# mLSTM cell followed by a leaky-ReLU MLP, in float32: the second product of the last group but one is computed by the same 26 block products as the last group's

## The chip, the cores and the metric

The kernel runs on one core of one Trainium2 chip. The time is the device time of one launch in microseconds (us). A core has TensorE (PE in the profile, its weight loads PEld), VectorE (DVE), ScalarE (ACT), GpSimd (POOL) and SyncE (SP, which only issues DMAs here). Each engine takes its instructions strictly in program order and they wait for one another through semaphores.

## The reference

```python
batch, n_heads, seq, head_dim = 4, 8, 768, 40        # q, k, v, o_gate; i_gate, f_gate without head_dim
for t in range(S):                                    # mLSTM cell
    m_new  = max(f_t + m, i_t); f_stab = exp(f_t + m - m_new); i_stab = exp(i_t - m_new); m = m_new
    C = f_stab * C + i_stab * outer(v_t, k_t)
    n = f_stab * n + i_stab * k_t
    y_t = sigmoid(o_t) * (C @ q_t) / max(abs(n . q_t), 1)
x = y as (3072 tokens, 320)                           # batch and time, heads and head_dim
h = x @ w_in                                          # 320 -> 2048
out = maximum(0.01 * h, h) @ w_out                    # 2048 -> 320
```

All data are float32.

## The kernel before

**Groups and stages.** The 768 time steps are cut into six chunks of 128. Chunk c of the four batches makes four *cells* (s = 4c to 4c + 3) and, afterwards, group c of the MLP: 512 tokens, one block of 128 per batch. The main loop (line 1471 onwards) runs stage c = 1 to 6: the MLP *units* of group c - 1 (`ffs = ff_units(c - 1)`), one per step i, and between them, at steps written out by hand, the pieces of the cells of chunk c. Stage 6 has no cells. So group 4's MLP runs beside the cells 20 to 23, and group 5's alone. All orders on TensorE, VectorE, ScalarE and GpSimd are those of the program text (`manual_schedule`).

**First product of a group** (`fast_firsts`, 14 units): x times w_in by seven products of half-size blocks (Winograd's form of Strassen's scheme) in two halves n each, in the order p1, p6, p7, p4, p2, p5, p3. The result of p1, p6, p7 is copied out by ScalarE (`keep`, line 1066); p2, p5, p3 add their PSUM banks to it on VectorE (`add`, line 1062, two instructions of 128x512 a unit), then ScalarE applies the leaky ReLU in place (`relu`, line 1058). p5 and p3 of a half share their PSUM banks: p3 goes on accumulating in them after p5's `add` has read them. The tiles of PSUM come from two pools of four banks, `psf` and `psc`, each handed round in order. The input sums for the next group (`sums_of_x`, line 1015, four on GpSimd) stand at the end of each stage.

**Second product.** Groups 1 to 4 use `fast_units`: 14 units, seven products of 8 float32 block matmuls in two halves, in all 112 of 128x128 by 128x160, each recorded as two (224 records). Group 5 uses `last_units`: activations in 4x4 blocks (a00 to a33, 512 rows of features, one batch), w_out in 4x2 blocks (b00 to b31, 512 by 160), output 4x2 (c00 to c31), and 26 products P0 to P25 instead of 32, each 4 block matmuls: 104 in all, 208 records. A text table says what each unit does: B are sums of blocks of w_out, A sums of activations, N and c the accumulations of the products. Two-operand lines go to VectorE (`nc.vector.tensor_tensor`, lines 1238 and 1246), a line that copies a product goes to ScalarE (1241, 1243). In group 5 the 18 sums B0 to B17 (128x640 each) are made by VectorE in the units 0 to 7 of the first product, after one instruction (line 1256) that adds back a half of w_out that Strassen's scheme had replaced by a difference.

**A cell of chunk 5** has two pieces on TensorE: `u_parts` (scores, matmuls of lines 725 and 731; then on VectorE four multiplications, line 742, and a state addition, 705) and `u_mix` (matmuls of line 813 into a bank pT; then on VectorE a transpose, line 820, three small denominators and a multiply, line 824; on GpSimd a multiply, line 827; on VectorE a second transpose, line 831; four DMAs to `x_dr`, and later `gather_x`, which reads them back as the next group's xT). Ahead of `u_parts`, VectorE transposes k and q (`prep_kq`, line 604, two instructions) and multiplies (line 612, two instructions). These four are taken from the generator `fine[s]`, one per unit. GpSimd makes a scaled state (701) and scaled k (567) per cell in `ahead`.

In stage 5, `pairs = (-1, -1, 3, 3, 13, 13, 17, 17, 17)` places the pieces: `u_parts` of cells 20 and 21 ahead of unit 0, their `u_mix` after unit 3, `u_parts` of 22 and 23 after unit 13, that is after the first product, and their `u_mix` after unit 17, inside the second.

Of the kernel before, what the change touches and what calls it, by code (L numbers as in the profile page):

```python
# [18 lines left out]
def kernel(  # L19
# [28 lines left out]
    P = 128  # L48
# [753 lines left out]
    def u_mix(s):  # L802

        c, b = divmod(s, B)
        d = st[s]
        prep_o(s)
        pT = psc.tile([P, PR * P], F32, name="pT", tag="c")
        S, m = S_t[s % NL], mixed(s)
        for u in range(2):
            for j in range(PR):  # L810
                for r in range(2):
                    h = 2 * j + r
                    nc.tensor.matmul(  # L813
                        pT[DP * r : DP * (r + 1), j * P + u * SL : j * P + (u + 1) * SL], lhsT=S[:, u, h, :],
                        rhs=m[:, u, h, :], start=True, stop=True,
                    )
        if c + 1 < NB:
            state_next(s, 1)
        hb = wk.tile([P, PR * TB, QW], F32, name="hb", bufs=1)
        nc.vector.transpose(hb[:].rearrange("p (j n) d -> p j n d", n=TB), in_blocks(pT[:]))  # L820
        den = wk.tile([P, PR * TB], F32, name="den")
        denominators(den[:], hb[:, :, DB])
        x3 = xb[:, :, :DB]
        nc.vector.scalar_tensor_tensor(  # L824
            x3, in0=raw_blocks(s, 2, DB), scalar=1.0, in1=hb[:, :, :DB], op0=ALU.add, op1=ALU.mult,
        )
        nc.gpsimd.tensor_tensor(x3, x3, den[:].unsqueeze(2).to_broadcast([P, PR * TB, DB]), op=ALU.mult)  # L827
        if c + 1 < NB:
            state_add(s, 1)
        xq = wk.tile([P, PR * P], F32, name="x")  # L830
        nc.vector.transpose(in_blocks(xq[:]), xb[:].rearrange("p (j n) d -> p j n d", n=TB))
        to = x_dr[s].rearrange("(j n i) t -> n i j t", n=4, i=DB)
        for n in range(4):
            sync.dma_start(to[n], xq[QW * n : QW * n + DB].rearrange("p (j t) -> p j t", t=P))
        del st[s]
# [30 lines left out]
    def ff_units(g):  # L866
# [45 lines left out]
        if g == NB - 1:  # L912
            return last_units(g, fast_firsts(g))
# [103 lines left out]
    def fast_firsts(g):  # L1017
# [94 lines left out]
    LAST_ROWS, LAST_KS = (0, 2, 1, 3), (1, 2, 0, 3)  # L1112
    LAST_EARLY = {
# [13 lines left out]
    }  # L1127
    LAST = (
# [26 lines left out]
    )  # L1155

    def last_units(g, firsts):
# [5 lines left out]
        lo = raw_l[:, : 3 * KH * NH]  # L1163
# [3 lines left out]
        flat = [t[:].rearrange("p n h d -> p (n h d)") for t in (kn, qn)]  # L1167
        flat += [t[:].rearrange("p u h d -> p (u h d)") for t in S_t]
        r_l = [t[:].rearrange("p u w -> p (u w)") for t in rb_t]
        sums_b = [lo[:, n * NW : (n + 1) * NW] for n in range(6)]  # L1170
        sums_b += [t[:, n * NW : (n + 1) * NW] for t in flat[:2] + r_l for n in range(3)]
        sums_b += [t[:, :NW] for t in flat[2:]]
        sums_a = [w_all[:, n, :AW] for n in range(NL)] + [t[:, :AW] for t in sums_b[18:]]
        del sums_b[18:]
        sums_a += [xb[:].rearrange("p n d -> p (n d)")]
        sums_c = [t[:, NW + n * NH :][:, :NH] for t in flat[2:] for n in range(2)] + p1_at
        behind = [w_all[:, n, AW:] for n in range(NL)]
        behind += [w_in[:, n, m * AW : (m + 1) * AW] for n in range(QN) for m in range(2)]
        text = "; ".join([LAST_EARLY[n] for n in sorted(LAST_EARLY)] + list(LAST))
        words = [w.strip("-") for w in text.replace(";", " ").split()]  # L1180
        left = {w: words.count(w) for w in words}
        spare = {"A": sums_a, "B": sums_b, "N": sums_c}
        tiles = {}

        def name(w):
# [3 lines left out]
            if kind == "a":  # L1189
                m, n = LAST_ROWS[int(rest[0])], LAST_KS[int(rest[1])]  # L1190
                return acts[:, 4 * n : 4 * n + 4, ts(m, P)]
            if kind == "b":
                n = LAST_KS[int(rest[0])]
                return w_out[:, 4 * n : 4 * n + 4, ts(int(rest[1]), NH)]
            if kind == "c":
                m = LAST_ROWS[int(rest[0])]
                return rows[m][:, ts(int(rest[1]), NH)]
# [3 lines left out]
            else:  # L1201
                got = spare[kind].pop(0)
                tiles[w] = got if kind == "N" else got.rearrange("p (f d) -> p f d", f=4)
            return tiles[w]

        def used(*ws):
            for w in ws:
                left[w] -= 1
                if left[w] == 0 and w[0] == "A":
                    spare["A"].append(tiles[w].rearrange("p f d -> p (f d)"))  # L1210
                if left[w] == 0 and w[0] == "N":
                    spare["N"].append(tiles[w])
# [5 lines left out]
        def send(w):  # L1218
            m, d = LAST_ROWS[int(w[1])], int(w[2])
            if w[:2] != "c2":  # L1220
# [4 lines left out]
            else:  # L1225
                cols = ts(d, NH)
            sync.dma_start(out[m * S + g * P : m * S + (g + 1) * P, cols], rows[m][:, cols])

        def do(line):
            to, op, *ws = line.split()  # L1230
            signed, ws = ws[0], [w.strip("-") for w in ws if w not in ("+", "-", "*")]
            src = [name(w) for w in ws]
            if op == "=" and " * " in line:
                bank = name(to)
                for f in range(4):
                    nc.tensor.matmul(bank, lhsT=src[0][:, f, :], rhs=src[1][:, f, :], start=f == 0, stop=f == 3)  # L1236
            elif len(src) == 2:
                nc.vector.tensor_tensor(name(to), src[0], src[1], op=ALU.add if " + " in line else ALU.subtract)
            elif op == "=":
                if signed[0] == "-":  # L1240
                    nc.scalar.activation(name(to), src[0], AF.Copy, scale=-1.0)
                else:
                    nc.scalar.copy(name(to), src[0])
            else:
                z = name(to)
                nc.vector.tensor_tensor(z, z, src[0], op=ALU.add if op[0] == "+" else ALU.subtract)
            used(to, *ws)

        def run_lines(lines):
            for line in lines.split(";"):  # L1250
                do(line.strip())

        def ahead_of(n):
            firsts[n]()
            if n == 0:
                nc.vector.tensor_tensor(low_w[:, :, NH:], low_w[:, :, NH:], low_w[:, :, :NH], op=ALU.add)
            if n in LAST_EARLY:
                run_lines(LAST_EARLY[n])

        def product(n):  # L1260
            if n == 0:
                sums_a.extend(behind)
            run_lines(LAST[n])

        return [lambda n=n: ahead_of(n) for n in range(len(firsts))] + [lambda n=n: product(n) for n in range(len(LAST))]
# [167 lines left out]
    with tc.manual_schedule(engines={E.PE, E.DVE, E.Activation, E.Pool}):  # L1433
# [31 lines left out]
        pairs = (-1, -1, 3, 3, 13, 13, 17, 17, 17)  # L1465
# [125 lines left out]
```

## Time and profile before

| what | value |
|---|---|
| median of 3 runs | 471.49 us (470.62 to 472.23) |
| the profiled execution | 471.96 us, of which the span of its instructions 470.2 us |
| PE busy | 459.6 us (98% of the span) |
| PEld busy | 412.5 us (88%) |
| DVE busy | 365.4 us (78%) |
| ACT busy | 206.6 us (44%) |
| POOL busy | 170.1 us (36%) |
| granted TensorE clock | 1.00 |

Times inside the text count from the start of the span. Stage 5 lies between 337.6 us (first `u_parts`) and 407.4 us; stage 6 from there to the end. A busy time is the union of an engine's instructions, and idle time of an engine that nobody waits for costs nothing; what matters is which wait ends last at each step of the chain.

### The profile page before, as it was taken

How to read it: one execution, taken by the hardware profiler on the slowest of the kernel's cores; microseconds unless marked ns; L12 is line 12 of the kernel's file. 1: busy time of each engine (PE TensorE's matmuls, PEld its weight loads, DVE VectorE, ACT ScalarE, POOL GpSimd, SP SyncE). 2: the span in 40 equal slices, each digit the busy share in tenths (PEclk: the TensorE clock that was granted, in tenths of full speed). 3: DMA queues.
4: the chain of work that ended last, by engine and by line, in shares of the span. 5: the costliest groups of instructions: out<-in, count | busy, mean ns of one | idle time of the engine just before them, and what ended most of it. 6: DMA issues, size and time to landing. Idle time of an engine off the chain costs nothing.

```text
span 470.2 us, 14195 instructions
## 1 busy us (share of the span) xinstructions
PE 459.6 (98%) x5700; PEld 412.5 (88%) x5700; DVE 365.4 (78%) x676; ACT 206.6 (44%) x507; POOL 170.1 (36%) x219
## 2 busy tenths in 40 slices
PE   8988989999999999999999999999999999999997
PEld 5777878767788999988899988899988899988997
DVE  6778578998579999768689778689757687495886
ACT  4657878755337511356411367411356411153410
POOL 6230487264335154933214933214833004400000
PEclk9999999999999999999999999999999999999999
DMA  9999977878742594865654956654776213100001
GB/s 128 169 179 179 214 181 230 207 158 164 147 141 55 151 181 107 186 141 134 166 133 84 197 127 140 179 110 100 176 142 125 75 30 85 57 1 1 1 1 56
DMA packets 160849, 59.21 MB, mean 126 GB/s; under 512 B 123792, under 2 KB 152208, under 8 KB 160784
## 3 DMA queue, kind: packets, MB, share of 16 engines
q1 hardware_dynamic: 120800, 51.15, 49.3%
q10 hardware_dynamic: 39984, 7.17, 9.3%
q8 instruction: 45, 0.74, 0.7%
q14 instruction: 20, 0.16, 0.1%
HBM read 51.58 MB, written 6.70 MB: 124 GB/s over the span
## 4 chain that ended last, share of the span: by engine, by line
PE 88%; DMA 5%; SPq 3%; POOL 1%; issue 1%; ACT 0%; DVE 0%; POOLq 0%; DVEq 0%
PE ph L1033 33%; PE po L931 26%; PE po L894 8%; PE pl L1236 6%; PE pT L813 3%; SPq L95 3%; PE ph L872 3%; PE sd L725 3%; DMA kn<-in_k_dram 3%; DMA acts<-in_moe_w_in_dram 1%; DMA w<-a_dr 1%; PE sd L731 1%; PE tk L638 1%; PE hN L785 1%; PE tkq L652 0%
## 5 line engine op out<-in xcount | busy, mean ns | idle before, releaser
L1033 PE MATMUL ph<-xT,w_in 64*128 64x256 f32 x720 | 82.7, 378 | 0.0
L1033 PEld LDWEIGHTS ph<-xT,w_in 64*128 64x128 f32 x720 | 69.2, 187 | 8.6 <-issue 0.6
L931 PE MATMUL po<-w_out,acts 128*128 128x160 f32 x512 | 71.3, 300 | 0.0
L931 PEld LDWEIGHTS po<-w_out,acts 128*128 128x128 f32 x512 | 69.9, 190 | 0.3
L1062 DVE TENSOR_TENSOR acts<-acts,ph 128x512 f32<-128x512 f32 x60 | 38.4, 683 | 22.8 <-PE ph L1033 22.7
L1066 ACT COPY acts<-ph 128x512 f32<-128x512 f32 x60 | 32.2, 588 | 49.7 <-PE ph L1033 49.7
L931 PE MATMUL po<-raw,acts 128*128 128x160 f32 x384 | 53.2, 300 | 0.0
L537 POOL TENSOR_SCALAR_AFFINE_SELECT w<-w 64x512 f32<-64x512 f32 x40 | 34.4, 861 | 51.3 <-DMA w<-a_dr 40.5
L931 PEld LDWEIGHTS po<-raw,acts 128*128 128x128 f32 x384 | 52.3, 190 | 0.3
L1058 ACT ACTIVATE acts<-acts 128x1024 f32<-128x1024 f32 x30 | 31.6, 1055 | 40.3 <-DVE acts L1062 30.8
L701 POOL TENSOR_TENSOR S<-S,f 40x336 f32<-40x336 f32 x36 | 30.6, 849 | 48.4 <-PE pT L813 32.7
L547 ACT ACTIVATE w<-w,gT 128x64 f32<-128x64 f32 x160 | 41.6, 337 | 13.1 <-DMA a_dr<-a 4.2
L742 DVE TENSOR_TENSOR qn<-w,sd 64x384 f32<-64x384 f32 (+1 forms) x80 | 33.4, 418 | 14.7 <-ACT acts L1066 7.8
L872 PE MATMUL ph<-xT,w_in 64*128 64x256 f32 x320 | 37.8, 383 | 0.0
L894 PE MATMUL po<-w_out,acts 128*128 128x320 f32 x128 | 36.7, 437 | 0.0
L1033 PE MATMUL ph<-acts,w 64*128 64x256 f32 x320 | 36.3, 379 | 0.0
L827 POOL TENSOR_TENSOR xb<-xb,den 128x320 f32<-128x320 f32 x16 | 11.6, 728 | 67.0 <-DVE xb L824 64.7
L872 PEld LDWEIGHTS ph<-xT,w_in 64*128 64x128 f32 x320 | 31.5, 187 | 3.8 <-ACT acts L880 0.4
L1033 PEld LDWEIGHTS ph<-acts,w 64*128 64x128 f32 x320 | 30.6, 187 | 3.6
L894 PEld LDWEIGHTS po<-w_out,acts 128*128 128x128 f32 x128 | 23.5, 190 | 9.2 <-ACT acts L880 0.3
L612 DVE TENSOR_TENSOR qn<-kqT,ea 64x512 f32<-64x512 f32 x32 | 30.0, 938 | 0.8
L1033 PE MATMUL ph<-xT,raw 64*128 64x256 f32 x240 | 26.8, 376 | 0.0
(267 smaller groups left out, 807.2 us busy)
## 6 DMA issues: line engine op xcount, KB each, us to landing
rb<-in_k_dram SPq DMA_DIRECT2D x64, 80.0 KB
rb<-in_q_dram SPq DMA_DIRECT2D x64, 80.0 KB
rb<-in_o_gate_dram SPq DMA_DIRECT2D x64, 80.0 KB
ea<-a_dr SPq DMA_DIRECT2D x32, 128.0 KB
raw<-in_moe_w_out_dram SPq DMA_DIRECT2D x6, 640.0 KB
w<-a_dr ACTq DMA_DIRECT2D x24, 128.0 KB
x_dr<-x SPq DMA_DIRECT2D x64, 40.0 KB
xT<-x_dr SPq DMA_DIRECT2D x16, 160.0 KB
```

What stands on the lines that cost most here:

```text
L537: nc.gpsimd.affine_select(part, part, compare_op=ALU.is_ge, fill=-1e30, base=0, pattern=[[0, H], [1, SL]], channel_multiplier=-1,)
L547: yield nc.scalar.activation(w[:, h, :], w[:, h, :], AF.Exp, bias=gT[c][:, 0, bh : bh + 1], scale=1.0)
L612: nc.vector.tensor_tensor(mixed(s)[rows, 1 - r], d["kqT"][rows, 1].rearrange("p (h t) -> p h t", t=SL), d["ea"][rows], op=ALU.mult,)
L701: nc.gpsimd.tensor_tensor(new, old, g, op=ALU.mult)
L742: nc.vector.tensor_tensor(mixed(s)[toks, u, hs], w[toks, hs], bank[1 - u][to[u][hs.start], hs], op=ALU.mult,)
L872: nc.tensor.matmul(ph[r][:, cols], lhsT=w_row(r, slot, j), rhs=xT[DP * r : DP * (r + 1), slot, cols], start=(slot == 0), stop=(slot == KC ...
L894: nc.tensor.matmul(po[n][:], lhsT=acts[:, f, ts(n, P)], rhs=w_out[:, f, :], start=(f == 0), stop=(f == NF - 1),)
L931: nc.tensor.matmul(bank[:], lhsT=left[:, f, :], rhs=right[:, f, :], start=f == 0, stop=f == KH - 1)
L1033: nc.tensor.matmul(bank[r][:, e, :], lhsT=left(r)[rows, e], rhs=right(r)[rows], start=first and e == 0 and m == 0, stop=e == 1 and m == le ...
L1058: nc.scalar.activation(to, z, AF.Prelu, alpha=0.01)
L1062: nc.vector.tensor_tensor(to[:, 2 * r : 2 * r + 2], to[:, 2 * r : 2 * r + 2], bank[r], op=ALU.add)
L1066: nc.scalar.copy(to[:, 2 * r : 2 * r + 2], bank[r])
```

## The change

`last_units` becomes `sum_units`, with one table for group 4 and one for group 5. Group 4's second product takes 26 units instead of 14. Since stage 5 now makes the sums of w_out, group 5 takes them over (`weight_sums` is shared) and its first product has only A0 to A4 left to make. In group 4, line "restore", B0, B1 and B2 stay on VectorE (unit 1); the other 15 sums are given to GpSimd (`by Pool:`), in units 2 to 12 and 14. The A sums A0 to A4 are made in units 11 to 13, A5 to A27 in the second product. The tiles for the sums are borrowed from buffers of cells that are done, and from the places of b00 and b11.

The cells of stage 5 move: `u_parts` of 22 and 23 from after unit 13 to after unit 9, their `u_mix` from after unit 17 to after unit 13, with the `fine` steps taken two at a time at units 4, 5, 7 and 8. `u_mix` is cut in three: matmuls, `gated` (lines 820 to 827) and `turned` (line 831 and the DMAs). For cell 22 `gated` stays at unit 13 and `turned` comes in unit 16 (table entry "mix 0"), followed there by cell 23's `gated` and by the gather of 22; cell 23's `turned` and gather come in unit 19 ("mix 1").

```diff
+        def gated():
             ...   (hb transpose, denominators, multiply, GpSimd's multiply)
+        def turned():
             ...   (second transpose, four DMAs to x_dr)
+        if s < NS - 2:
+            gated()
+            turned()
+        elif s == NS - 2:
+            gated()
+            tails.append([turned, lambda: gather_x(s)])
+        else:
+            tails[0].insert(1, gated)
+            tails.append([turned, lambda: gather_x(s)])
...
-        if g == NB - 1:
-            return last_units(g, fast_firsts(g))
+        if g >= NB - 2:
+            return sum_units(g, fast_firsts(g))
...
+    SUM_ROWS = {NB - 2: (3, 0, 2, 1), NB - 1: (0, 2, 1, 3)}
+    SUM_EARLY = {
+        NB - 2: {
+            1: "restore; B0 = b10 - b11; B1 = b21 + B0; B2 = b00 + b30",
+            2: "by Pool: B3 = B2 - b10; by Pool: B4 = B1 + B3",
+            3: "by Pool: B5 = b10 - B1",
+            6: "by Pool: B6 = b11 - b31",
+            7: "by Pool: B7 = b01 - B6",
+            8: "by Pool: B8 = B1 - b20; by Pool: B9 = b00 - b01",
+            9: "by Pool: B10 = b30 + B9; by Pool: B11 = B10 - b31",
+            10: "by Pool: B12 = b10 - B6; by Pool: B13 = B12 - b30",
+            11: "by Pool: B14 = b20 + B9; by Pool: B15 = B7 + B14; A0 = a10 - a12",
+            12: "by Pool: B16 = b01 + B14; A1 = a21 + a23; A2 = a11 + a31",
+            13: "A3 = a01 - A1; A4 = a02 - a32",
+        },
...
+    SUM_UNITS = {
+        NB - 2: (
+            "P0 = A3 * B4; by Pool: B17 = B14 - b21",
+            "P1 = A1 * B5; N0 = -P0; A5 = a10 + a20",
+            "P2 = a31 * b10; c21 = P1; mix 0",
+            "P3 = A5 * B7; c30 = P2; N1 = -P2",
+            "P4 = A0 * b20",
+            "P5 = a30 * b01; A6 = a00 + A3; c10 = -P4; N2 = P4; N0 += P1; mix 1",
+            "P6 = A4 * B8; c31 = P5; N3 = P5",
+            "P7 = a03 * B11; A7 = A6 - a30; N4 = -P6; A8 = A5 - a23",
+            "P8 = A7 * B2; c21 += P3; c01 = -P7; A9 = A8 + A2; A10 = A0 - a32",
...
+            "P24 = A25 * b21; c20 -= N5; N0 += N5; c30 += P21; c01 += N0",
+            "P25 = A27 * B0; N4 += N0; c20 -= P22; c00 += N4; c20 += N4; c21 += P24; c20 += P23; N9 -= P25; c11 += N9; c31 -= N9",
+        ),
...
+                elif line.startswith("by Pool: "):
+                    do(line[len("by Pool: ") :], nc.gpsimd)
...
+        last_pairs = (-1, -1, 3, 3, 9, 9, 13, 13)
...
-                at = place if c == 1 else first_pairs if c == 2 else pairs
+                at = place if c == 1 else first_pairs if c == 2 else pairs if c + 1 < NB else last_pairs
...
-                for _ in range(1 if c > 1 and i < N1 else 2 if i > 5 else 0):
+                for _ in range((2 if i in (4, 5, 7, 8) else 0) if c == NB - 1 and i > 3 else 1 if c > 1 and i < N1 else 2 if i > 5 else 0):
```

More of the change, by code (lines that the diff above doesn't have):

```diff
@@ L818, in u_mix @@
             state_next(s, 1)
[L819 to L835, printed above, removed]
+        def gated():
+            hb = wk.tile([P, PR * TB, QW], F32, name="hb", bufs=1)
+            nc.vector.transpose(hb[:].rearrange("p (j n) d -> p j n d", n=TB), in_blocks(pT[:]))
+            den = wk.tile([P, PR * TB], F32, name="den")
+            denominators(den[:], hb[:, :, DB])
+            x3 = xb[:, :, :DB]
+            nc.vector.scalar_tensor_tensor(
+                x3, in0=raw_blocks(s, 2, DB), scalar=1.0, in1=hb[:, :, :DB], op0=ALU.add, op1=ALU.mult,
+            )
+            nc.gpsimd.tensor_tensor(x3, x3, den[:].unsqueeze(2).to_broadcast([P, PR * TB, DB]), op=ALU.mult)
+            if c + 1 < NB:
+                state_add(s, 1)
+        def turned():
+            xq = wk.tile([P, PR * P], F32, name="x")
+            nc.vector.transpose(in_blocks(xq[:]), xb[:].rearrange("p (j n) d -> p j n d", n=TB))
+            to = x_dr[s].rearrange("(j n i) t -> n i j t", n=4, i=DB)
+            for n in range(4):
+                sync.dma_start(to[n], xq[QW * n : QW * n + DB].rearrange("p (j t) -> p j t", t=P))
+            del st[s]
+        if s < NS - 2:
[7 more added lines that the diff above has]
+            tails.append([turned, lambda: gather_x(s)])
     def gather_x(s):
@@ L1110, in fast_firsts, with sum_units @@
         return [lambda p=p, n=n: p(n) for p in order for n in range(2)]
-    LAST_ROWS, LAST_KS = (0, 2, 1, 3), (1, 2, 0, 3)
-    LAST_EARLY = {
[13 rows of a table removed]
-    }
-    LAST = (
[26 rows of a table removed]
-    )
-    def last_units(g, firsts):
-        lo = raw_l[:, : 3 * KH * NH]
+    SUM_KS = (1, 2, 0, 3)
+    SUM_ROWS = {NB - 2: (3, 0, 2, 1), NB - 1: (0, 2, 1, 3)}
+    SUM_EARLY = {
+        NB - 2: {
[11 rows of a table added]
+        },
+        NB - 1: {
+            8: "A0 = a01 - a21",
+            9: "A1 = a21 + a23",
+            10: "A2 = a01 - A1",
+            11: "A3 = a11 + a31",
+            12: "A4 = a13 + A3",
+        },
+    }
+    SUM_UNITS = {
+        NB - 2: (
[26 rows of a table added]
+        ),
+        NB - 1: (
[26 rows of a table added]
+        ),
+    }
+    weight_sums, tails = {}, []
+    def sum_units(g, firsts):
+        last = g == NB - 1
+        at_row, units, early_sums = SUM_ROWS[g], SUM_UNITS[g], SUM_EARLY[g]
         rows = [wk.tile([P, Dm], F32, name="y")[:] for _ in range(2)]
@@ L1166, in last_units @@
         NW, AW = 4 * NH, 4 * P
-        flat = [t[:].rearrange("p n h d -> p (n h d)") for t in (kn, qn)]
-        flat += [t[:].rearrange("p u h d -> p (u h d)") for t in S_t]
+        k_l, q_l = (t[:].rearrange("p n h d -> p (n h d)") for t in (kn, qn))
+        s_l = [t[:].rearrange("p u h d -> p (u h d)") for t in S_t]
         r_l = [t[:].rearrange("p u w -> p (u w)") for t in rb_t]
-        sums_b = [lo[:, n * NW : (n + 1) * NW] for n in range(6)]
-        sums_b += [t[:, n * NW : (n + 1) * NW] for t in flat[:2] + r_l for n in range(3)]
@@ L1172, in last_units, with plain @@
[L1172 to L1179, printed above, removed]
+        def plain(w):
+            n = SUM_KS[int(w[1])]
+            return w_out[:, 4 * n : 4 * n + 4, ts(int(w[2]), NH)]
@@ new lines, in sum_units @@
+        homes = [raw_l[:, n * NW : (n + 1) * NW] for n in range(6)] + [k_l[:, :NW], s_l[0][:, :NW], s_l[1][:, :NW]]
+        homes += [k_l[:, n * NW : (n + 1) * NW] for n in (1, 2)] + [t[:, n * NW : (n + 1) * NW] for t in r_l for n in range(2)]
+        homes = [t.rearrange("p (f d) -> p f d", f=4) for t in homes]
+        homes += [plain(w) for w in ("b00", "b11")] + [q_l[:, :NW].rearrange("p (f d) -> p f d", f=4)]
+        once = x4_at.rearrange("p k t -> p (k t)")
+        sums_a = [w_all[:, n, :AW] for n in range(NL)]
@@ new lines, in sum_units @@
+        later_a = [t[:, n * AW : (n + 1) * AW] for t in s_l[2:] for n in range(2)]
+        later_a += [t[:, 2 * RW : 2 * RW + AW] for t in r_l[: 2 if last else 1]]
+        if last:
+            sums_a += [q_l[:, NW + n * AW :][:, :AW] for n in range(2)] + later_a
+            later_a = [w_all[:, n, AW:] for n in range(NL)]
+            later_a += [w_in[:, n, m * AW : (m + 1) * AW] for n in range(QN) for m in range(2)]
+        else:
+            sums_a += [once]
+        sums_c = p1_at + [t[:, NW + n * NH :][:, :NH] for t in s_l[:2] for n in range(2)]
@@ L1180, in last_units @@
+        sums_c += [t[:, 2 * RW + AW :][:, :NH] for t in r_l[: 2 if last else 1]]
+        from_xb = [xb[:].rearrange("p n d -> p (n d)")[:, n * NH : (n + 1) * NH] for n in range(3)]
+        if last:
+            sums_c += from_xb
+        text = "; ".join([early_sums[n] for n in sorted(early_sums)] + list(units))
         words = [w.strip("-") for w in text.replace(";", " ").split()]
         left = {w: words.count(w) for w in words}
-        spare = {"A": sums_a, "B": sums_b, "N": sums_c}
-        tiles = {}
+        spare = {"A": sums_a, "B": homes, "N": sums_c}
@@ L1185, in name @@
+        tiles, homes_of = weight_sums, {}
         def name(w):
@@ L1189, in name @@
             if kind == "a":
-                m, n = LAST_ROWS[int(rest[0])], LAST_KS[int(rest[1])]
+                m, n = at_row[int(rest[0])], SUM_KS[int(rest[1])]
                 return acts[:, 4 * n : 4 * n + 4, ts(m, P)]
             if kind == "b":
-                n = LAST_KS[int(rest[0])]
-                return w_out[:, 4 * n : 4 * n + 4, ts(int(rest[1]), NH)]
+                return plain(w)
             if kind == "c":
-                m = LAST_ROWS[int(rest[0])]
-                return rows[m][:, ts(int(rest[1]), NH)]
+                return rows[at_row[int(rest[0])]][:, ts(int(rest[1]), NH)]
             if kind == "P":
@@ L1201, in name @@
             else:
-                got = spare[kind].pop(0)
-                tiles[w] = got if kind == "N" else got.rearrange("p (f d) -> p f d", f=4)
+                got = homes_of[w] = spare[kind].pop(0)
+                tiles[w] = got.rearrange("p (f d) -> p f d", f=4) if kind == "A" else got
             return tiles[w]
@@ L1208, in used @@
                 left[w] -= 1
[L1209 to L1212, printed above, removed]
+                if left[w] == 0 and w[0] in "ANP":
+                    t = homes_of.pop(w, None)
+                    tiles.pop(w)
+                    if t is not None and t is not once:
+                        spare[w[0]].append(t)
                 if left[w] == 0 and w[0] == "c":
@@ L1218, in send @@
         def send(w):
-            m, d = LAST_ROWS[int(w[1])], int(w[2])
-            if w[:2] != "c2":
+            m, d = at_row[int(w[1])], int(w[2])
+            cols = ts(d, NH)
+            if not last or w[:2] != "c2":
                 whole.add(w)
@@ L1224, in send, with do @@
                 cols = slice(0, Dm)
-            else:
[L1226 to L1246, printed above, removed]
+            sync.dma_start(out[m * S + g * P : m * S + (g + 1) * P, cols], rows[m][:, cols])
+        def do(line, eng):
+            to, op, *ws = line.split()
+            ws, minus = [w.strip("-") for w in ws if w not in ("+", "-", "*")], ws[0][0] == "-"
+            src = [name(w) for w in ws]
+            z = name(to)
+            if " * " in line:
+                for f in range(4):
+                    nc.tensor.matmul(z, lhsT=src[0][:, f, :], rhs=src[1][:, f, :], start=f == 0, stop=f == 3)
+            elif len(src) == 2:
+                eng.tensor_tensor(z, src[0], src[1], op=ALU.add if " + " in line else ALU.subtract)
+            elif op == "=" and minus:
+                nc.scalar.activation(z, src[0], AF.Copy, scale=-1.0)
+            elif op == "=":
+                nc.scalar.copy(z, src[0])
+            else:
+                eng.tensor_tensor(z, z, src[0], op=ALU.add if op[0] == "+" else ALU.subtract)
             used(to, *ws)
@@ L1250, in run_lines, with first @@
             for line in lines.split(";"):
-                do(line.strip())
-        def ahead_of(n):
+                line = line.strip()
+                if line == "restore":
+                    nc.vector.tensor_tensor(low_w[:, :, NH:], low_w[:, :, NH:], low_w[:, :, :NH], op=ALU.add)
+                elif line.startswith("mix "):
+                    n = int(line.split()[1])
+                    for fn in tails[n]:
+                        fn()
+                    if n == 0:
+                        sums_a.append(r_l[1][:, 2 * RW : 2 * RW + AW])
+                        sums_c.append(r_l[1][:, 2 * RW + AW :][:, :NH])
+                    else:
+                        sums_c.extend(from_xb)
+                elif line.startswith("by Pool: "):
+                    do(line[len("by Pool: ") :], nc.gpsimd)
+                else:
+                    do(line, nc.vector)
+        def first(n):
             firsts[n]()
[L1255 to L1258, printed above, removed]
+            if n in early_sums:
+                run_lines(early_sums[n])
         def product(n):
             if n == 0:
-                sums_a.extend(behind)
-            run_lines(LAST[n])
-        return [lambda n=n: ahead_of(n) for n in range(len(firsts))] + [lambda n=n: product(n) for n in range(len(LAST))]
+                sums_a.extend(later_a)
+            run_lines(units[n])
+        return [lambda n=n: first(n) for n in range(len(firsts))] + [lambda n=n: product(n) for n in range(len(units))]
     def u_gates(c):
@@ L1485, in visits @@
                     done += 1
-                    if fn is u_mix:
+                    if fn is u_mix and s < NS - 2:
                         waiting.append(s)
```

80 rows, old and new, of tables (LAST, LAST_EARLY, SUM_UNITS) are left out of this document.

## The prediction

> **What bounds the kernel now.** I read the page first (PE busy for 98% of the span, DVE 78%), then the chain of work that ended last from 320 us on, in order of time. Columns: start, length, line, instructions.
>
> ```profile
> 339.34 7.11 PE ph L1033 x64
> 346.44 2.02 PE pT L813 x64
> 348.46 24.37 PE ph L1033 x224
> ...
> 374.58 8.89 PE po L931 x64
> 383.48 2.02 PE pT L813 x64
> 385.49 21.93 PE po L931 x160
> 407.42 31.28 PE ph L1033 x288
> 438.70 28.46 PE pl L1236 x208
> ```
>
> The chain is TensorE without a gap. Between the third row and the fourth stands `u_parts` of cells 22 and 23, 372.83 to 374.58, 1.75 us. The fourth and sixth rows are group 4's second product, 30.82 us for 224 records; the last row is the scheme that is to replace it, 28.46 us for 208. The waits in this stretch put no wait on another engine before TensorE. So what TensorE saves counts, as long as the others stay ahead of it. How far ahead they are is read from the busy times by stage (stage 5's second product, then stage 6's):
>
> ```profile
> 374.60:407.40 32.80, 32.80 (x290) 32.39 (x290) 20.96 (x37) 3.71 (x11) 12.01 (x12) 1.00 0.23 65
> 438.70:467.50 28.80, 28.45 (x209) 28.21 (x208) 24.30 (x61) 6.02 (x19) 0.00 (x0) 1.00 0.04 15
> ```
>
> The numbers after the length are PE, PEld, DVE, ACT, POOL. Beside the 26 products VectorE is busy for 24.30 of 28.80 us, with nothing else to do and GpSimd silent. That is the row that the change must be held against: in stage 5 there are cells too, and GpSimd works. What the two do to each other shows where `prep_kq`'s multiplications meet the input sums:
>
> ```profile
> 335.30 0.68 DVE L612 TENSOR_TENSOR qn<-kqT,ea 64x512 f32<-64x512 f32 x1
> 335.91 0.30 DVE L990 TENSOR_TENSOR y<-y,po 128x160 f32<-128x160 f32 x1
> 336.25 1.42 DVE L612 TENSOR_TENSOR qn<-kqT,ea 64x512 f32<-64x512 f32 x1
> ```
>
> ```profile
> 335.53 1.59 POOL L1015 TENSOR_TENSOR acts<-xT 128x512 f32<-128x512 f32 x1 [1.67 <-DMA rb<-in_o_gate_dram]
> 337.20 1.61 POOL L1015 TENSOR_TENSOR xT<-xT 128x512 f32<-128x512 f32 x1
> 338.88 1.27 POOL L1015 TENSOR_TENSOR acts<-xT 128x512 f32<-128x512 f32 x1
> ```
>
> The second multiplication takes 1.42 us instead of 0.68: it ends 0.55 us after GpSimd's sum ends at 337.12, so it did not run beside it, but behind it. The first sum in turn took 1.59 us instead of 1.27, as it waited for the multiplication that ended at 335.98. L990, which has one input in PSUM, was not held up.
>
> **The change part by part.**
>
> *TensorE.* 28.46 for 30.82 us: -2.36. The cells' matmuls only change places (1.75 and 2.02 us). Were TensorE never to wait, P0 would begin at 339.34 + 7.11 + 2.02 + 24.37 + 1.75 + 2.02 = 376.6.
>
> *GpSimd's price.* No 128x640 sum of GpSimd's is shown. Its 128x512 takes 1.27 us and its 128x160 (L974) 0.52 when nothing holds them up: 0.75 us for 352 elements, so 1.27 + 0.27 = 1.55 us. Below, 1.27 (it can't be cheaper than the smaller one); above, the held-up 1.60 x 640/512 = 2.0. I take 1.55, the nearer row.
>
> *B3, B4, B5 stand ahead of cell 20's GpSimd multiply.* VectorE is free from 343.1 to 347.57, and the same four instructions (restore, B0, B1, B2) took 407.70 to 411.5 in stage 6, so B2 is there at 346.9 at no cost. Then GpSimd: 346.9 + 3 x 1.55 + 0.73 (L827) = 352.3. Queued behind it: on VectorE cell 20's second transpose, until now at 350.36, and all after it. Now 4.7 us lie from that transpose to the first `prep_kq` transpose (355.04); it comes at 357.0, 2.0 us later.
>
> *VectorE from there to A3 is one queue.* Transposes 4 x 0.66 = 2.7; multiplications 4 x 0.65 = 2.6; the adds of p2, p5, p3, 1.2 a unit; `u_parts`' multiplications and additions of both cells 4.4 (374.06 to 378.46 in the timeline of before), which until now lay behind all adds and now lie ahead of p5's. So p5(0)'s adds end at 357.0 + 2.7 + 2.6 + 2.4 + 4.4 + 1.3 = 370.4. p3(0) may not overwrite that bank earlier, and TensorE would be there at 369.4 (348.46 + 24.37 x 176/224 + 1.75): 1.0 us of wait. After it VectorE follows TensorE by its own adds and A3, and P0 begins at 377.7. Cost without hold-ups: +1.1 us (bounds 0, with sums of 1.3 us, to +2.5 with sums of 2.0).
>
> *Hold-ups ahead of P0.* From 358 to 377 GpSimd runs B6 to B16 back to back (11 x 1.55 = 17 us). In this stretch VectorE has seven instructions with both inputs in SBUF that the queue depends on: four multiplications, A0, A1, A2. Each finds a sum running and waits for what is left of it: on average half, 0.75 us, at most 1.5. I take six of them: +4.5 us (bounds 0 and 10). The adds, with one input in PSUM, go free. The Trainium skill (SBUF — State Buffer, "Who interferes with whom") says that a VectorE instruction with two SBUF inputs contends with a GpSimd instruction that reads SBUF, and that the later one blocks for the whole instruction. The trace agrees (1.42 us beside 0.68, the PSUM row at 0.30); by the rule taken at its worst, seven whole sums, the term would be 10.9 in place of 4.5 and the sum 483.6.
>
> *Second product.* The A sums and accumulations (23 and 36 instructions, as many as in group 5's) are 24.30 - 1.3 (the last adds) = 23.0 us of VectorE. New beside them: `gated` 22 and 23 (1.9 each by 384.61 to 386.48) and `turned` (1.0 each): 5.8, in all 28.8 against TensorE's 28.46. So there is nothing in reserve, and what holds VectorE up shows in the end: B17 and two multiplies (1.55 + 2 x 0.73), then the four `sums_of_x` (1.27 each, at 400.21 now, when VectorE idles), which now fall among A20 to A27 since x is earlier. Bounds 0 and 8; an A is made some units ahead of its product, which hides much, so +2.5 us, as gaps ahead of late products and of group 5's first unit, which needs the banks of P19 and P21.
>
> *At nothing.* ScalarE copies (0.29 us each, 3.71 us busy in 32.8). Group 5's first product loses 18 instructions of VectorE (0.82), which lay under TensorE's 31.28 us: no gain. SP's queue is passed by the x DMAs earlier, with nothing behind them that is due. `u_parts` four units sooner needs the v loads of cell 23, issued by ScalarE up to 354.78 for the half that it reads, 8 us ahead; the other half up to 361.24, 11 us ahead of `u_mix`. If that cover fails, a microsecond or two.
>
> Sum: -2.36 + 1.1 + 4.5 + 2.5 = +5.7 us on the profiled 471.96, its span 470.2 and 1.8 around it: 477.7. That execution was 0.5 above the median of 471.49, so on the median 477.2.
>
> **The rivals.**
> 1. *VectorE keeps up, faster.* If a GpSimd sum costs 1.3 us and the instructions of both interleave without waiting, A3 is ready when TensorE gets to P0, and -2.36 + 0.4 is left: 469.5. It decides at 376.6: if A3 ends earlier, the scheme pays. For it: VectorE idles 12 us between adds in stage 5's first product now. Against it: the 1.42 us row, and the 2.0 us that B3 to B5 cost ahead of everything.
> 2. *Sums at 1.55 but no hold-ups:* -2.36 + 1.1 = -1.3, 470.2, which is no difference. Against it, the same row.
> 3. *Hold-ups only ahead of P0,* the second product absorbs its own: -2.36 + 1.1 + 4.5 = +3.2, 474.7. For it: the A sums in group 5's second product are up to some units early.
> 4. *Long sums:* at 2.0 us B3 to B5 add another 1.4 and each of six hold-ups 0.22 more: 479.9.
>
> **How the numbers follow.** About 0.3% (1.4 us) is what a measurement of this kernel can tell from no change. Forecast 0.48 and 477.2; rival 4, 0.10; rival 3, 0.14; rival 2, 0.11; rival 1, 0.17. So faster 0.17, same 0.11, slower 0.72. The range leaves out rival 1 and the far end of the hold-ups: 470.2 (rival 2) to 481.5 (the forecast with the hold-ups ahead of P0 at 8.8, near their bound). The slower cases' own range is 474 to 481.5.
>
> **What would show it.** In the profile after: 208 records of pl instead of 224 of po, at about 28.5 us when not waiting (TensorE's term). GpSimd's 128x640 sums at 1.5 to 2.1 us, and cell 20's second transpose near 352.3 (GpSimd's price). A0 to A2 and L612 at over 0.7 us (hold-ups). In the waits, TensorE behind VectorE's adds of p5 ahead of p3, and behind A3 ahead of P0, which begins near 382. Group 5's first unit near 413. P0 by 377 with A0 to A2 at 0.68 would make the forecast wrong; so would a late bank or a late v load as the longest wait.

## The result and the profile after

The kernel after takes 476.8 us (median of 6 runs, 476.65 to 478.68); the kernel before, in runs beside it, 471.5 us. The ratio is 1.0125, with a 95% interval of 1.0104 to 1.0146: 5.3 us slower. The forecast was 477.2 us, slower. The profiled execution of after took 476.84 us, its span is 475.0 us; before it was 471.96 and 470.2, so the profiles differ by 4.8 us.

Lines of `kernel.py` move with the change: the matmul of a first product is L1047 now (it was L1033), the matmul of the 26 products L1303 (L1236), the sums A and B L1305 on either engine (L1238), the accumulations L1311 (L1246), the adds of the first product L1076 (L1062), the multiplies and transposes of `u_mix` L826, L829 and L835 (L824, L827, L831), `sums_of_x` L1029 (L1015).

The page's chain of work that ended last, by engine:

```profile
PE 73%; DVE 9%; SPq 7%; issue 3%; DMA 3%; POOL 3%; ACT 0%; POOLq 0%; DVEq 0%
```

By the page TensorE is still busy for 97% of the span, and that figure hides the whole matter. In the chain before, nothing but TensorE stood from 339 us on. Now VectorE has 9% of the chain, and the same stretch of it, in order of time (start, length, engine, line, instructions), reads:

```profile
348.60 6.29 PE ph L1047 x56
...
370.61 0.61 DVE acts L1076
...
371.26 3.05 PE ph L1047 x22
...
375.62 3.39 DVE w L1305 x2
...
399.21 1.45 DVE S L1305
400.66 1.31 DVE y L1311
...
412.03 31.48 PE ph L1047 x285
443.51 28.46 PE pl L1303 x208
```

The chain leaves TensorE at 355 us, comes back to it for 3 us in p3, and then stays on VectorE and GpSimd until 412.03, where group 5's first product resumes. The last two rows are group 5, from where its first product resumes, at the pace of before. The waits that TensorE has in this stretch (us in total, times, longest) follow; before had none.

```profile
PE pl L1303 <- DVE w L1305: 1.8, 1, 1.8
PE ph L1047 <- DVE acts L1076: 1.5, 1, 1.5
PE ph L1047 <- DVE y L1311: 1.1, 1, 1.1
PE pl L1303 <- DVE S L1305: 0.4, 1, 0.4
```

From the top these are: P0 behind A3; p3 behind the adds of p5; group 5's first unit behind the accumulation that reads P21's bank; and P8 behind its A sum. VectorE's timeline shows what lies behind the first three of them:

```profile
349.57 1.52 DVE L826 SCALAR_TENSOR_TENSOR xb<-rb,hb 128x320 f32<-128x320 f32 x1
353.21 1.10 DVE L835 STREAM_TRANSPOSE x<-xb 128x512 f32<-128x512 f32 x1 [2.12 <-POOL xb L829]
...
359.11 1.86 DVE L612 TENSOR_TENSOR qn<-kqT,ea 64x512 f32<-64x512 f32 x2
...
375.54 3.48 DVE L1305 TENSOR_TENSOR w<-acts 128x512 f32<-128x512 f32 x2
...
380.13 0.83 DVE L1305 TENSOR_TENSOR w<-acts,w 128x512 f32<-128x512 f32 x1
...
399.11 1.55 DVE L1305 TENSOR_TENSOR S<-raw,w 128x512 f32<-128x512 f32 x1
400.58 1.39 DVE L1311 TENSOR_TENSOR y<-y,S 128x160 f32<-128x160 f32 x1
401.89 1.79 DVE L1305 TENSOR_TENSOR S<-S,acts 128x512 f32<-128x512 f32 x1
403.60 0.31 DVE L1311 TENSOR_TENSOR raw<-raw,pl 128x160 f32<-128x160 f32 x1
```

And on GpSimd beside them:

```profile
349.16 1.58 POOL L1305 TENSOR_TENSOR raw<-raw 128x640 f32<-128x640 f32 x1
350.70 1.79 POOL L1305 TENSOR_TENSOR raw<-w_out,raw 128x640 f32<-128x640 f32 x1
352.45 0.73 POOL L829 TENSOR_TENSOR xb<-xb,den 128x320 f32<-128x320 f32 x1
...
374.96 1.54 POOL L1305 TENSOR_TENSOR rb<-w_out,kn 128x640 f32<-128x640 f32 x1
376.58 1.88 POOL L1305 TENSOR_TENSOR w_out<-S,rb 128x640 f32<-128x640 f32 x1
...
398.66 1.45 POOL L1029 TENSOR_TENSOR acts<-xT 128x512 f32<-128x512 f32 x1 [10.08 <-DMA xT<-x_dr]
```

Three things are to be seen. Cell 20's second transpose, at 353.21, has waited for L829, which stands behind B3, B4 and B5 on GpSimd; and the multiply L826 ahead of it took 1.52 us beside B4, where it took 0.49 in the kernel before. A1 and A2 take 3.48 us together instead of 1.29: A1 ends behind the sum that runs to 376.50, A2 behind the one that runs from 376.58 to 378.46. And the sums of x, which ran while VectorE idled before, now begin at 398.66 in a stretch where VectorE has no idle time at all: A sums of 0.70 us take 1.55 and 1.79, an accumulation of 0.32 us with both inputs in SBUF takes 1.39, while L1311 with one input in PSUM stays at 0.31. In the kernel before, the first sum of x and the VectorE instruction beside it read:

```profile
400.21 1.27 POOL L1015 TENSOR_TENSOR acts<-xT 128x512 f32<-128x512 f32 x1
```

```profile
401.01 0.32 DVE L985 TENSOR_TENSOR hn<-hn,po 128x160 f32<-128x160 f32 x1 [3.80 <-PE po L931]
```

VectorE had been idle for 3.80 us there, and its instruction, with one input in PSUM, took 0.32.

### The profile page after: what moved, and what is told of

Its sections match the earlier page's. It is cut to its first block, busy times and chain, and to the rows that moved or that the text cites. A ratio compares the mean times of both kernels' runs of the same rounds, so it can differ in the third digit from the quotient of the medians.

```text
span 475.0 us, 14224 instructions
## 1 busy us (share of the span) xinstructions
PE 462.5 (97%) x5684; PEld 413.8 (87%) x5684; DVE 376.5 (79%) x709; ACT 209.6 (44%) x517; POOL 194.0 (41%) x228
## 4 chain that ended last, share of the span: by engine, by line
PE 73%; DVE 9%; SPq 7%; issue 3%; DMA 3%; POOL 3%; ACT 0%; POOLq 0%; DVEq 0%
PE ph L1047 30%; PE po L945 19%; PE po L908 8%; SPq L95 7%; PE pl L1303 6%; PE pT L813 3%; PE sd L725 3%; PE ph L886 2%; DMA a_dr<-a 2%; DVE S L1305 2%; DVE w L1305 2%; DVE acts L1076 1%; PE sd L731 1%; DMA ea<-a_dr 1%; DVE y L1311 1%
## 5 line engine op out<-in xcount | busy, mean ns | idle before, releaser
L1047 PE MATMUL ph<-xT,w_in 64*128 64x256 f32 x720 | 84.7, 378 | 1.1 <-DVE y L1311 1.1
L1047 PEld LDWEIGHTS ph<-xT,w_in 64*128 64x128 f32 x720 | 70.7, 187 | 9.6 <-DVE y L1311 1.5
L1076 DVE TENSOR_TENSOR acts<-acts,ph 128x512 f32<-128x512 f32 x60 | 38.3, 682 | 30.7 <-PE ph L1047 30.6
L537 POOL TENSOR_SCALAR_AFFINE_SELECT w<-w 64x512 f32<-64x512 f32 x40 | 36.5, 912 | 52.1 <-DMA w<-a_dr 41.2
L945 PE MATMUL po<-w_out,acts 128*128 128x160 f32 x384 | 53.5, 300 | 0.0
L945 PEld LDWEIGHTS po<-w_out,acts 128*128 128x128 f32 x384 | 52.4, 190 | 0.2
L886 PE MATMUL ph<-xT,w_in 64*128 64x256 f32 x320 | 39.9, 399 | 0.0
L945 PE MATMUL po<-raw,acts 128*128 128x160 f32 x288 | 39.9, 300 | 0.0
L945 PEld LDWEIGHTS po<-raw,acts 128*128 128x128 f32 x288 | 39.2, 190 | 0.2
L886 PEld LDWEIGHTS ph<-xT,w_in 64*128 64x128 f32 x320 | 32.8, 195 | 4.3 <-PE ph L886 0.3
L1047 PE MATMUL ph<-acts,w 64*128 64x256 f32 x320 | 36.5, 379 | 0.0
L1047 PEld LDWEIGHTS ph<-acts,w 64*128 64x128 f32 x320 | 31.1, 187 | 3.4
L908 PEld LDWEIGHTS po<-w_out,acts 128*128 128x128 f32 x128 | 23.5, 190 | 9.2 <-ACT acts L894 0.3
L612 DVE TENSOR_TENSOR qn<-kqT,ea 64x512 f32<-64x512 f32 x32 | 30.9, 964 | 0.8
L1047 PE MATMUL ph<-xT,raw 64*128 64x256 f32 x240 | 27.7, 377 | 1.5 <-DVE acts L1076 1.5
L1047 PEld LDWEIGHTS ph<-xT,raw 64*128 64x128 f32 x240 | 23.8, 187 | 4.6 <-DVE acts L1076 2.2
```

What stands on the lines that cost most here:

```text
L537: nc.gpsimd.affine_select(part, part, compare_op=ALU.is_ge, fill=-1e30, base=0, pattern=[[0, H], [1, SL]], channel_multiplier=-1,)
L886: nc.tensor.matmul(ph[r][:, cols], lhsT=w_row(r, slot, j), rhs=xT[DP * r : DP * (r + 1), slot, cols], start=(slot == 0), stop=(slot == KC ...
L908: nc.tensor.matmul(po[n][:], lhsT=acts[:, f, ts(n, P)], rhs=w_out[:, f, :], start=(f == 0), stop=(f == NF - 1),)
L945: nc.tensor.matmul(bank[:], lhsT=left[:, f, :], rhs=right[:, f, :], start=f == 0, stop=f == KH - 1)
L1047: nc.tensor.matmul(bank[r][:, e, :], lhsT=left(r)[rows, e], rhs=right(r)[rows], start=first and e == 0 and m == 0, stop=e == 1 and m == le ...
L1076: nc.vector.tensor_tensor(to[:, 2 * r : 2 * r + 2], to[:, 2 * r : 2 * r + 2], bank[r], op=ALU.add)
```

## The experiments

All edits but one are to the kernel after; times are medians, ratios are to the kernel before on the same chip (472.09 us for the first four, 471.72 for the other three).

**GpSimd's sums left out.** B3 to B17 are not made; the products that use them read B0's tile in their place.

```diff
-                    do(line[len("by Pool: ") :], nc.gpsimd)
+                    to, _, *ws = line[len("by Pool: ") :].split()
+                    ws = [x for x in ws if x not in ("+", "-")]
+                    for x in ws:
+                        name(x)
+                    tiles[to] = tiles["B0"]
+                    used(to, *ws)
```

> The changed kernel without the 15 sums that GpSimd makes; the products read B0 in their place (this part of the computation is left out). Theory 1 (GpSimd's sums hold VectorE up: three of them stand ahead of cell 20's multiply, the others hold the shared access to SBUF): P0 at 377, group 5's first unit near 407, time 471.5 to 472.5, some 5 us less than the change. Theory 2 (VectorE's own load is too much, cells and A sums and accumulations, whatever GpSimd does): at most 1 us less than the change, 475.8 or more.

Measured: 473.75 us, ratio 1.0033 (1.0015 to 1.005); the profiled execution took 472.29 us with a span of 470.4 us, 4.6 less than after. The median lies between the two ranges that were expected, above 471.5 to 472.5 and below 475.8; the profiled execution lies in the first, with P0 at 376.51 and group 5's first unit resumed at 407.49, as theory 1 had them. In VectorE's timeline A1 and A2 are back at their own price, and TensorE's waits ahead of p3 and P0 are gone:

```profile
373.08 1.29 DVE L1305 TENSOR_TENSOR w<-acts 128x512 f32<-128x512 f32 x2
```

```profile
PE ph L1047 <- DVE y L1311: 1.1, 1, 1.1
PE pl L1303 <- DVE S L1305: 0.3, 1, 0.3
```

The second fence is the waits of TensorE from 335 us on. So the two large waits come from GpSimd's sums of w_out, and the one ahead of group 5 does not.

**Sums that only write.** Each sum on GpSimd becomes three memsets of its tile (the 15 sums are not computed), which keep GpSimd busy and read nothing.

```diff
+                    for _ in range(3):
+                        nc.gpsimd.memset(name(to), 0.0)
```

> In the place of each of GpSimd's 15 sums stand three memsets of the same tile (the sums are left out, the products read zeros), about 1.9 us of GpSimd that reads nothing from SBUF. Theory 1: what holds VectorE up is GpSimd's reading. A0 to A3 and L612 go back to about 0.68 us, which gives back 3 us; B3 to B5 stand ahead of the cell's multiply as before and cost up to 1 us more. Time 474 to 475. Rival (any GpSimd instruction holds VectorE up, or GpSimd is late as an engine): A1 and A2 still at 1.3 us or more, time 476.5 or more.

Measured: 475.27 us, ratio 1.0076 (1.0048 to 1.0104), just above the 474 to 475 that were expected; span 472.2. GpSimd's and VectorE's timelines around P0:

```profile
345.46 5.92 POOL L1334 MEMSET raw<- 128x640 f32 x9
...
369.15 7.87 POOL L1334 MEMSET rb<- 128x640 f32 x12
```

```profile
352.22 1.10 DVE L835 STREAM_TRANSPOSE x<-xb 128x512 f32<-128x512 f32 x1 [3.13 <-POOL xb L829]
...
374.54 1.29 DVE L1305 TENSOR_TENSOR w<-acts 128x512 f32<-128x512 f32 x2
```

Three memsets take about 2.0 us, more than a free sum's 1.54. GpSimd runs memsets without a pause from 369.15 to 377.02, and A1 and A2, in the middle of them, take 1.29 us. Most of the delay of cell 20's transpose stays, and with it a wait ahead of p3 (1.0 us by the waits, as the prediction had it, where after has 1.5); the wait ahead of P0 is gone. (That the transpose comes at 352.22, close to the 352.3 of the prediction, is in part luck: the nine memsets in the place of B3 to B5 are longer than the sums, but begin at 345.46, as they don't wait for B2.) It is GpSimd's reading that holds VectorE up, and its mere occupation that makes L829 late. That is the rule of the Trainium skill (SBUF — State Buffer, "Who interferes with whom") that a VectorE instruction with two SBUF inputs contends with one of GpSimd that reads SBUF and not with one that only writes it; the two timelines, 3.48 us and 1.29 us, agree.

**No sums of x in stage 5.** `sums_of_x` for group 5 is left out; its first product reads what lies in the tiles.

```diff
-                if i == n_ff - 1 and c < NB:
+                if i == n_ff - 1 and c < NB - 1:
```

> The changed kernel without group 5's four input sums on GpSimd (left out; the products of group 5 read older sums). Theory 1: the gap of 1.4 us in group 5's first unit and part of its slow start go, as VectorE's last accumulations end about 4 us sooner; 1.5 to 2.5 us less than the change, 474.3 to 475.3. Theory 2 (VectorE is late there by its own 59 instructions): under 0.5 us less.

Measured: 476.38 us (473.02 to 478.94), ratio 1.0086 (1.0052 to 1.012); above the 474.3 to 475.3 that were expected, and by the times alone it can't be told from after. The trace shows what changed: the wait ahead of group 5 is gone, and its first product takes 31.28 us to the first record of the second product, as before, instead of 33.18. What this profiled execution gained there it lost elsewhere; the windows around p3 (length; PE, PEld, DVE, ACT, POOL busy; granted clock; DMA) show it:

```profile
370.00:371.00 1.00, 0.26 (x1) 0.26 (x2) 1.00 (x3) 0.00 (x0) 1.00 (x2) 1.00 0.00 0
371.00:372.00 1.00, 1.00 (x6) 0.66 (x7) 1.00 (x3) 0.68 (x1) 1.00 (x1) 0.82 0.00 0
372.00:373.00 1.00, 1.00 (x8) 0.75 (x7) 1.00 (x2) 0.86 (x2) 0.92 (x2) 0.50 0.05 16
...
375.00:376.00 1.00, 1.00 (x12) 0.84 (x10) 0.50 (x1) 0.00 (x0) 0.98 (x1) 0.97 0.00 0
```

The granted clock is at one half for about 3.4 us, from 371.64 on, 0.9 us after the wait ahead of p3 ended at 370.74, and p3's 48 records take 7.73 us instead of 6.04. Two of the six runs of after (478.18 and 478.68, mean clock 0.996) may hold such a dip too; they have no profile.

**B3, B4, B5 two units later,** behind both cells' GpSimd multiplies.

```diff
-            2: "by Pool: B3 = B2 - b10; by Pool: B4 = B1 + B3",
-            3: "by Pool: B5 = b10 - B1",
+            4: "by Pool: B3 = B2 - b10; by Pool: B4 = B1 + B3; by Pool: B5 = b10 - B1",
```

> The changed kernel with B3, B4 and B5 made in unit 4, behind the multiplies and states of cells 20 to 23, and not in units 2 and 3. Theory 1: cell 20's second transpose is back near 350.5 and VectorE's queue 2 us sooner, of which 1 us is kept since the later sums then meet more of VectorE's instructions: 475.3 to 476.2, TensorE's wait for p5's adds down from 1.7 to about 0.5 us. Rival (that delay is hidden): no change, the wait ahead of p3 stays at 1.5 us.

Measured: 477.65 us, ratio 1.0123 (1.01 to 1.0146): no gain, against what was expected. Cell 20's transpose was back at 350.51 and the wait ahead of p3 was gone. But GpSimd's sums then lay later against VectorE's queue (VectorE's timeline, then TensorE's two longest; the lines are one lower here):

```profile
370.99 1.09 DVE L1304 TENSOR_TENSOR w<-acts 128x512 f32<-128x512 f32 x1
373.58 3.92 DVE L1304 TENSOR_TENSOR w<-acts 128x512 f32<-128x512 f32 x2
...
379.38 2.03 DVE L1304 TENSOR_TENSOR raw<-acts 128x512 f32<-128x512 f32 x1
```

```profile
PE pl L1302 <- DVE w L1304: 2.6, 1, 2.6
PE pl L1302 <- DVE S L1304: 2.0, 2, 1.4
```

A0, A1 and A2 lose 3.0 us (5.01 for 0.68 + 1.29), and A4, behind P0's A3, 1.35: the waits ahead of P0 and in the second product grew by 0.8 and 1.6 us. What the sooner transpose gave came back as hold-ups.

**All 18 sums on VectorE.** GpSimd makes none.

```diff
-                    do(line[len("by Pool: ") :], nc.gpsimd)
+                    do(line[len("by Pool: ") :], nc.vector)
```

> The changed kernel with all 18 sums of w_out on VectorE, at the same places in the order; GpSimd makes none. Theory 1, with the addition that VectorE's queue is the scarce thing however it is filled: no instruction of VectorE is held up ahead of P0, but 15 sums of 0.74 us (11 us) stand in the queue, against the 3 us of hold-ups and the 1.4 us behind B3 to B5 that go: the wait ahead of p3 grows to 4 us, P0 comes at 385, time 479 to 481. Rival (contention is the whole matter, VectorE has 12 us to spare in the first product): 473 to 474.5, as the write-only kernel or better.

Measured: 481.74 us, ratio 1.0219 (1.0191 to 1.0247), slightly more than expected. A1 and A2 take 1.29 us, but 15 instructions of 0.82 us stand in VectorE's queue. TensorE's longest wait:

```profile
PE ph L1047 <- DVE acts L1076: 3.8, 2, 3.6
```

p3 waits 3.6 us, and here too the clock drops to one half behind that wait (0.56 and 0.59 in the windows 376 to 378 and 378 to 380 us), with p3's 48 records at 7.73 us. So at these places in the order GpSimd was the better engine for the sums; neither is free.

**Only the cells moved.** The kernel before, with `last_pairs` and the `fine` steps of the change and nothing else.

```diff
+        last_pairs = (-1, -1, 3, 3, 9, 9, 13, 13)
...
-                at = place if c == 1 else first_pairs if c == 2 else pairs
+                at = place if c == 1 else first_pairs if c == 2 else pairs if c + 1 < NB else last_pairs
...
-                for _ in range(1 if c > 1 and i < N1 else 2 if i > 5 else 0):
+                for _ in range((2 if i in (4, 5, 7, 8) else 0) if c == NB - 1 and i > 3 else 1 if c > 1 and i < N1 else 2 if i > 5 else 0):
```

> The kernel before, with one part of the change alone: the last pair of cells four units sooner, and the steps of prep_kq two at a time. Theory 1: VectorE's queue reaches the end of p5's adds at 368.4, ahead of TensorE at 369.4, so no wait and no difference, 471.5 to 472.5. Rival (4.4 us of VectorE's work for u_parts ahead of p5's adds make TensorE wait by themselves, and the v loads are late): TensorE waits 1 to 2 us ahead of p3 or in u_parts, 473 to 474.5.

Measured: 472.01 us, ratio 0.9998 (0.9983 to 1.0013), and TensorE waits nowhere in the stretch. Moving `u_parts` and `u_mix` costs nothing by itself.

**The scheme alone.** The edits of the first and the third experiment together: neither GpSimd's sums of w_out nor group 5's sums of x are made.

> The changed kernel without GpSimd's 15 sums and without group 5's four input sums (both left out), so that the 26 products and VectorE's part are left. Theory 1: TensorE waits for under 1 us in all; what TensorE saves is seen, -2.36 + about 0.8, and the time is 1.0 to 1.8 us below the kernel before. Theory 2 (VectorE's own load beside the cells is too much): still over the kernel before.

Measured: 470.50 us, ratio 0.9969 (0.9953 to 0.9986): faster than before, by 1.5 us by the ratio and 1.2 by the medians. One wait is left:

```profile
PE pl L1303 <- DVE S L1305: 0.3, 1, 0.3
```

Three of these kernels stand between before and after as steps. The time from the first record of cell 20's `u_parts` to TensorE's last product, in the profiled executions:

| kernel | what GpSimd does in stage 5 | us | step |
|---|---|---|---|
| before | sums of x, while VectorE idles | 129.65 | |
| the scheme alone | neither sums of w_out nor of x | 128.14 | -1.51 |
| no sums of w_out | sums of x, while VectorE is full | 130.26 | +2.12 |
| sums that only write | and is busy ahead of L829 | 132.10 | +1.84 |
| after | and reads SBUF beside L826, A1, A2 | 134.31 | +2.21 |

The steps add up to +4.66 us, of the 4.8 by which the spans differ. The ratios give the same order and the same end, with other steps between (0.9969, 1.0033, 1.0076, 1.0125: -1.5, +3.0, +2.0, +2.3 us). The second step is 1 us larger by them, and the clock accounts for most of that: of the twelve runs without the sums of w_out, the six with a mean granted clock of 0.993 took 473.78 to 474.96 us, the six at 0.999 or 1.00 took 472.19 to 473.72. By the medians of the runs at 0.999 or 1.00 alone, of these two kernels and of before beside each, the second step is 2.0 us. Where in the kernel the clock fell in the others isn't shown; they have no profile.

No version here that does the whole work is faster than the kernel before: the 1.5 us are there only with GpSimd's sums taken out.

## Why the prediction was right, step by step

**TensorE's term** (-2.36). 208 records of `pl`; where it doesn't wait, group 5's 28.46 us. The kernel with the scheme alone kept 1.5 of it. Most of the rest lies in the second product, 29.00 us there instead of 28.46, with a wait of 0.3; the prediction had that inside its second-product term.

**GpSimd's price** (1.55). Eight of the 15 sums took 1.54 to 1.58 us, the other seven 1.79 to 2.28; the mean is 1.75. B3 to B5 took 4.9 us together, near the forecast 4.65, and rival 4, which had 6.0 for them, falls with that.

**B3 to B5 ahead of L827** (transpose at 352.3 forecast, 353.21 measured). B4 and the multiply L826 of cell 20 met (1.52 us for the multiply, 0.49 before), and B5 took 1.79. The 1.1 us of the forecast, without hold-ups, is the fourth row of the table: 1.84. The wait itself was as computed, 1.0 us, where GpSimd only writes. What the prediction lacked is that p3, after the wait, took longer: 48 records in 6.04 us instead of 5.35 in the kernel without the sums. Where GpSimd reads, the transpose came 1.0 us later still and the wait ahead of p3 was 1.5: about 0.4 us of the table's last step belong here, 2.2 us in all.

**Hold-ups ahead of P0** (+4.5 forecast, bounds 0 and 10). This is the mis-sized term: the wait ahead of P0 is 1.8 us, the rest of the table's last step. Of the seven instructions, A1 and A2 lost 2.19 us, and one of the four L612 0.06; A0 lost nothing: it was the sum beside it, recorded as begun 0.20 us sooner, that took longer, 2.28 us. A3, which was not among the seven, lost 0.15, since the sums ran on to 380.41 and not to 377. The pair of L612 at 359.11 took 1.86 us, but not because of the sums: it took 1.87 in the kernel without them, and the kernel before has the same pair at the same price, in a line that the prediction doesn't use,

```profile
356.36 1.85 DVE L612 TENSOR_TENSOR qn<-kqT,ea 64x512 f32<-64x512 f32 x2
```

where GpSimd's scaled k and state, of the cells themselves, stand beside it. The error was to give each of six instructions the average of half a sum. Two were hit, but for 1.1 us each; beside the others it was GpSimd that waited, or neither.

**P0** was to begin near 382 and began at 381.10, against 376.6 without waits: 4.5 late instead of 5.6.

**Second product and group 5's start** (+2.5). The product takes 29.17 us, 0.7 more than 28.46; group 5's first product, counted the same way, takes 33.18 instead of 31.28, 1.9 more, and both experiments without the sums of x bring it back to 31.28. Together 2.6. The place was as forecast, at the end and by the sums of x: they hold VectorE up by (1.55 - 0.70) + (1.39 - 0.32) + (1.79 - 0.70) + (1.53 - 0.70) = 3.8 us, of which 1.9 reached TensorE there. Group 5's first unit resumed at 412.03 (413 forecast).

**The sum**: -2.36 + 2.2 + 1.8 + 2.6 = +4.2 us, and 0.14 us by which stage 5 began later anyway, against +4.8 of the spans (0.4 us are assigned to nothing); +5.7 was forecast. Two errors of the forecast offset each other in part: hold-ups ahead of P0 too long by 2.7, the delay of B3 to B5 too short by 1.1. The runs put the difference at 5.3 us, the profiles at 4.8: before's profiled execution was 0.5 above its median, after's was at it. So the places and the order of the costs were right, and that 477.2 came within 0.4 us of 476.8 is in part luck.

**The rivals.** Rival 1 had its point of decision in A3 ending before 376.6; it ended at 380.96. Its time, 469.5, is 1.0 us below what the scheme alone gives (470.50), so it came nearer to that kernel than to this one. Rival 2 fell with A1 and A2. Rival 3, hold-ups ahead of P0 only, comes to 474.7 and fell with the 1.9 us at group 5's start. Of "nothing" that was claimed for the moved cells, the kernel with the cells alone shows it: no wait, ratio 0.9998.

## What to carry to other kernels

Work given to GpSimd while it idles isn't free where it reads SBUF beside a full VectorE: count which of VectorE's instructions have two inputs in SBUF, look up in the trace which of them are already held up, and price the rest one by one by where the other engine's work lies, not by an average. Count also what stands behind the new work in the idle engine's own queue (here one 0.73 us multiply, behind three sums). And where the queue is full, moving the cost can give it back, as B3 to B5 two units later did. What paid here was work taken out; the sums of x cost TensorE no wait in the kernel before, where VectorE idles, but no run moved the sums of w_out to such a place.

## What the runs showed of the hardware that was not expected

A wait of TensorE in a first product cost more than its idle time. After 1.5 us ahead of p3, TensorE's windows show 4 matmul records in the first 0.74 us, where its pace is 12 a us, and p3 took 0.7 us longer; after the 1.1 us ahead of group 5, that product was 1.9 us longer in all. For p3 the weight loads of after show why:

```profile
371.26 0.29 PEld L1047 LDWEIGHTS ph<-xT,raw 64*128 64x128 f32 x2 [1.91 <-DVE acts L1076]
371.85 5.04 PEld L1047 LDWEIGHTS ph<-xT,raw 64*128 64x128 f32 x46 [0.30 <-DVE acts L1076]
```

A unit writes two PSUM banks by turns, one matmul each, and VectorE frees them by two adds, one after the other. Two weight loads go when the first add ends, and the other 46 go 0.59 us later, when the second does; that is most of the 0.7. Group 5's first unit has the same form: two records at 410.27, the rest from 412.03 on. So the price of such a wait runs to the second bank's add, and the row of the waits shows only part of it.

In two profiled executions the granted clock also fell to one half for about 3.4 us behind such a wait (the windows of the kernels without sums of x and with all sums on VectorE), which made p3 1.7 us longer. The waits were 1.5 and 3.6 us. The Trainium skill (TensorE: Matmul & The Clock Gate, Part 1: The HAM clock gate) has the clock fall after at least one idle window of some 3.4 us. The length of the dip agrees with that window; the idle time ahead of it was less in the first case, 1.5 us. What set the dips off isn't shown: after's own profile, with the same wait, stays at 1.00 there, and has a dip at another place, 6.8 us at one half from 28.9 us on, while TensorE is recorded as busy.
